# Another order for the second batch's loads, and the last batch's tokens in their own order

## The chip, the cores and the metric

The kernel runs on one core of a Trainium2 chip. A core has a matrix engine (TensorE, PE in the profile), a vector engine (VectorE, DVE), a scalar engine (ScalarE, ACT), a general engine (GpSimd, POOL) and a queue engine (SyncE, SP). Each engine works through a list of instructions of its own, in order, and waits on semaphores for the others. Transfers run on sixteen DMA engines; here POOL, SP and ACT issue them. Matrix results land in PSUM, all else lives in SBUF. The metric is the device time of one execution in microseconds (us); lower is better.

## The reference

Eight batches of eight heads, 576 tokens and a head size of 64. Thirty-two packing queries `p` per head first attend to the tokens, then the tokens attend to the 32 packed rows, and the result goes through a two-layer network with a smoothed ReLU.

```python
p_packed = sm_attn(p, k, v)              # softmax(p k^T / 8) v: 32 rows per head
out = sm_attn(q, p_packed, p_packed)     # softmax(q p_packed^T / 8) p_packed
x = out.transpose(0, 2, 1, 3).reshape(B * S, H * D)      # 4608 tokens x 512
h = x @ w_in                                              # 2048 wide
g = where(h >= 1, h, where(h <= -1, 0, (h + 1)**2 / 4))
return g @ w_out                                          # 4608 x 512, f32
```

All inputs and the output are f32; the kernel computes in bf16 with f32 sums.

## The kernel before, in words

The attention's last product and the first layer are joined. For each batch the packed rows (`ppT`) are multiplied with `w_in` (the tile `M`, made in four quarters `M0` to `M3` from the PSUM tile `mp`, L493), and the normalised second softmax (`A`) is multiplied with `M`, which gives a hidden tile `h` of 128 features by 576 tokens directly (L548). There are sixteen hidden tiles per batch. ACT and DVE turn each into `hT` in three passes (L553, L558 or L560, L563). The second layer runs for pairs of batches: 1152 tokens are nine output tiles `o` of 128 tokens, each a sum of sixteen output steps (L598), copied to `ob` and written by SP (L604). The last output tile is copied and written in two halves of its columns, one by ACT and one by DVE and SP (L612).

The attention of one batch runs like this. `k` and `q` are turned so that the head size lies on the partitions: in batches 0 to 2 by matrix transposes into PSUM (`tp`, L376) and copies to `kT` and `qT`, from batch 3 on by transposing DMAs that SP issues (L512). `scores` (L397) multiplies `kT` with `pT`, ACT takes the exp (L400), and `packed` (L417, L423) multiplies with `v` and sums. DVE and ACT then make `ppT` (copy, add, copy) and `rs` (reciprocals). In batch 0 `packed` runs once for each half of the heads, in all other batches once for both. `weights` multiplies `ppT` with `qT` (L451), takes the second exp into `eT` (L456), sums over the rows (`sm`, L461), takes the logarithm and its exp (L465, L469) and multiplies to `A` (L472). Heads 0 to 3 and 4 to 7 are the two groups of all this.

Loads are issued by POOL (L259 for k, q and v, which are converted to bf16 on the way; L285 and L287 for quarters of `w_in` and `w_out`). A load puts six neighbouring tokens on one partition, that is, partition p holds the tokens 6p to 6p + 5. So a batch's columns stand by token mod 6 first, and then by token div 6, and the rows of an output tile are written to `out` with a step of six rows, in pieces of up to 96 (`out_rows`).

The order of all instructions is written by a planner in the kernel (`Plan`) when the program is built. Each piece of work is a task with engines, a cost (the table `C`), a key and what it depends on; the planner keeps a clock for each engine, and gives each engine in turn the task that it can start first, or one with a smaller key if it can start nearly as soon. A task with two engines goes to the one that it thinks will end it first. Loads go out in the order in which they were added. PSUM has three wide buffers (`W`, used by `tp`, `sp`, `pk`, `s`, `sm`, `mp` and `h`) and two for output tiles (`O`), given out in rotation; a task that writes one waits for the readers of the old content. While fewer than three `O` buffers have been taken and PE has nothing to do, the planner lets it multiply zeros (L661). The costs only decide the order; at run time the engines wait on semaphores for what really happens.

```python
add_weights("in", 0); add_weights("in", 1); add_weights("out", 0); add_weights("in", 2)
add_weights("out", 1); add_weights("in", 3); add_weights("out", 2)
add_load("k", 1, 2); add_load("v", 1, 1); add_load("q", 1, 2)
add_weights("out", 3)
```

This is the order of the loads after those of batch 0 (here with several calls on a line): `add_load(name, batch, parts)`.

Of the kernel before, what the change touches and what calls it, by code (L numbers as in the profile page):

```python
# [8 lines left out]

C = dict(load=2.95, half=1.46, w_in=2.57, w_out=2.57, rest=1.25, out=9.0, p=4.05, land=1.75, xt=5.0, xland=11.0,
         tpp=0.06, tp=0.042, sc=0.034, pk=1.05, s2=0.25, sm=0.245, M=0.345, h=0.49, o=0.217, switch=0.05, join=0.15,
         pTc=0.1, Tca=1.12, Tcd=0.76, ex=0.82, ppT=0.42, ppo=0.41, ppa=0.4, ppd=0.2, rs=0.18, eT=0.74, ln=0.65, rc=0.68, A=0.82,
         Mca=1.0, Mcd=1.22, x=0.65, ta=0.683, td=0.457, hT=0.758, oba=0.585, obd=0.69,
# [17 lines left out]
class Plan:  # L33
# [15 lines left out]
    def add(self, engines, cost, key, deps, fn, takes=None, readers=0, frees=None, mode=None, slack=None, after=0.0,  # L49
            holds=0.0):  # L50
        engines = (engines,) if isinstance(engines, str) else engines
        t = Task(engines, cost if isinstance(cost, dict) else {e: cost for e in engines}, key, deps, fn, takes, readers,
                 frees, mode, slack, after, holds)
        t.seq = len(self.tasks)
        self.tasks.append(t)
        return t
# [124 lines left out]
def kernel(  # L181
# [10 lines left out]
    nc = tc.nc  # L192
    f32 = mybir.dt.float32
    bf16 = mybir.dt.bfloat16
    AF = mybir.ActivationFunctionType
    ALU = mybir.AluOpType

    B, H, S, D = q.shape
# [3 lines left out]
    P = 128  # L202
    assert d_model == H * D and n_tokens == B * S
    assert S == 576 and D == 64 and NP == 32 and H == 8 and d_ff == 2048 and B % 2 == 0
    scale = 1.0 / math.sqrt(D)
# [3 lines left out]
    G = 2  # L209
    Q = 4  # L210
    TP = 96
    NC = S // TP
    X = 2
    E = NC // X
    HALF = S // X
    KF = d_ff // P
    FW = 512
    NF = d_ff // FW
# [15 lines left out]
    PE, ACT, DVE, DMA, SP = "PE", "ACT", "DVE", "DMA", "SP"  # L234
# [42 lines left out]
    def add_load(nm, b, parts=1, deps=(), cost="load"):  # L277
        for i, hs in enumerate([ALL] if parts == 1 else HS):
            L[nm, b, i] = add(DMA, C[cost] / parts, -1, deps, lambda nm=nm, b=b, hs=hs: load(nm, b, hs))
        if parts == 1:  # L280
            L[nm, b, 1] = L[nm, b, 0]

    def add_weights(which, f):
        if which == "in":
            fn = lambda: nc.gpsimd.dma_start(w_in_sb[:, :, f * FW:(f + 1) * FW], w_in_v[:, :, f * FW:(f + 1) * FW])  # L285
        else:
            fn = lambda: nc.gpsimd.dma_start(w_out_sb[:, 4 * f:4 * f + 4], w_out_v[:, 4 * f:4 * f + 4])  # L287
        L[which, f] = add(DMA, C["w_" + which], -1, (), fn)
# [8 lines left out]
            load(nm, 0, HS[i])  # L297
    for nm, i in FIRST:
        L[nm, 0, i] = add(DMA, C["half"], -1, (), (lambda: None) if L else first_loads)
    add_weights("in", 0)  # L300
    add_weights("in", 1)
    add_weights("out", 0)
    add_weights("in", 2)
    add_weights("out", 1)
    add_weights("in", 3)
    add_weights("out", 2)
    add_load("k", 1, 2)
    add_load("v", 1, 1)
    add_load("q", 1, 2)
    add_weights("out", 3)  # L310
    L["p"] = add(DMA, C["rest"], -1, (), lambda: nc.gpsimd.dma_start(p_nat[:, PB * 2:], p_v[:, PB * 2:]))


# [43 lines left out]
    def attention(b, key):  # L357
# [46 lines left out]
        def packed(gs, deps):  # L404
            box, ky = {}, key["pk" + str(gs[0])]
            hs, n = slice(Q * gs[0], Q * gs[-1] + Q), Q * len(gs)
            part = 0.55 if len(gs) < G else 1.0

            def mm():
                pk = wide([P, 1024], f32, "pk")  # L410
                vt, ex_ = tok["v", b], ex()
                v_ = box["v"] = pk[:, :n * X * NP].rearrange("p (h y) -> p h y", h=n)
                for g in gs:
                    for a in range(Q):
                        h = head(g, a)
                        for e in range(E):
                            nc.tensor.matmul(v_[:, h - hs.start].rearrange("p (x n) -> p x n", x=X),  # L417
                                             vt[:, h, X * e:X * (e + 1)].rearrange("p c d -> p (c d)"), ex_[:, e, g, :, a],
                                             start=(e == 0), stop=(e == E - 1))
                s_ = box["s"] = pk[:, 512:512 + 2 * len(gs)].rearrange("p (g y) -> p g y", y=2)  # L420
                for i, g in enumerate(gs):
                    for c in range(NC):
                        nc.tensor.matmul(s_[:, i], ex_[:, c // X, g, c % X].rearrange("p a n -> p (a n)"), ones2[:TP],  # L423
                                         start=(c == 0), stop=(c == NC - 1))
            t = add(PE, C["pk"] * len(gs) / G, ky, [L["v", b, g] for g in gs] + deps + old("s2", "M", "A"), mm, takes="W",
                    readers=3, mode=0)
            war = old("s2", "M")

            def odd(eng):
                box["p1"] = att.tile([D, n, NP], f32, tag="p1", name="p1")  # L430
                copy(box["p1"], box["v"][D:, :, NP:])(eng)
            c1 = both(odd, C["ppo"] * part, C["ppo"] * part, ky, [t] + war, frees=t)
            c2 = add(DVE, C["ppT"] * part, ky, [c1] + war, lambda eng: nc.vector.tensor_tensor(
                ppT()[:D, hs], box["v"][:D, :, :NP], box["p1"], ALU.add), frees=t)
            res = [c2, both(lambda eng: copy(ppT()[D:, hs], ppT()[:D, hs])(eng), C["ppa"] * part, C["ppd"] * part, ky, [c2] + war)]
            r = add(DVE, C["rs"], ky, [t] + old("eT", "A"), lambda eng: nc.vector.reciprocal(
                rs()[:, gs[0]:gs[-1] + 1], box["s"]), frees=t)
            return t, res, r
# [4 lines left out]
        def weights(g, deps, r):  # L443
            box, ky, km = {}, key["s2" + str(g)], key["sm" + str(g)]

            def mm():
                s2 = box["s2"] = wide([P, X, FW], f32, "s2")
                for a in range(Q):
                    h = head(g, a)
                    for x in range(X):  # L450
                        nc.tensor.matmul(s2[a * NP:(a + 1) * NP, x, :HALF], pp_of(x, h),  # L451
                                         qT()[x * D:(x + 1) * D, g, h % 4 * E * TP:][:, :E * TP], start=True, stop=True)

            def exp2(eng):
                box["eT"] = att.tile([P, X, HALF], bf16, tag="eT", name="eT")
                nc.scalar.activation(box["eT"], box["s2"][:, :, :HALF], AF.Exp, scale=rs()[:, g, 1:])  # L456

            def mm2():
                sm = box["sm"] = wide([P, X, FW], f32, "sm")
                for x in range(X):  # L460
                    nc.tensor.matmul(sm[:, x, :HALF], onesblk, box["eT"][:, x], start=True, stop=True)  # L461

            def ln(eng):
                box["ln"] = att.tile([P, X, HALF], f32, tag="ln", name="ln", bufs=1)
                nc.scalar.activation(box["ln"], box["sm"][:, :, :HALF], AF.Ln)  # L465

            def inv(eng):
                box["rc"] = att.tile([P, X, HALF], f32, tag="rc", name="rc")
                nc.scalar.activation(box["rc"], box["ln"], AF.Exp, scale=-1.0)  # L469

            def norm(eng):
                nc.vector.scalar_tensor_tensor(A()[:, g], box["eT"], rs()[:, g, :1], box["rc"], ALU.mult, ALU.mult)  # L472
            p_ = K.get((b - 1, "A" + str(g)), [])
            t, j = yield ky, C["s2"], deps + p_, mm
            e_ = add(ACT, C["eT"], ky, [t, r] + p_, exp2, frees=(t, j))
            t2 = add(PE, C["sm"], km, [e_], mm2, takes="W", readers=1, mode=0)
            l_ = add(ACT, C["ln"], km, [t2] + last.get("ln", []), ln, frees=t2)
            i_ = add(ACT, C["rc"], km, [l_] + p_, inv)
            a_ = add(DVE, C["A"], km, [i_] + K.get((b - 2, "h"), []), norm)
            last["ln"] = [i_]  # L480
            K[b, "A" + str(g)] = [a_]
            yield t, e_, a_
# [39 lines left out]
        s1, e1 = scores(1, kc1 + pT_of[b])  # L522
        q0, qc0 = trans("q", 0, qT, old("s2"))
        q1, qc1 = trans("q", 1, qT, old("s2"))
        pk, pc, r = zip(*([packed((0,), [e0]), packed((1,), [e1])] if b == 0 else [packed((0, 1), [e0, e1])] * G))
        K[b, "sc"], K[b, "pk"] = [s0, s1], list(pk)
        K[b, "kt"], K[b, "qt"] = [k0, k1], [q0, q1]
        ws, ms = [weights(g, pc[g] + (qc0, qc1)[g], r[g]) for g in range(G)], [mk(f, pc[0] + pc[1]) for f in range(NF)]
# [44 lines left out]
    def out_rows(pr, i):  # L573
        res, t = [], i * P
        while t < (i + 1) * P:
            b, x, e, r = 2 * pr + t // S, t % S // HALF, t % HALF // TP, t % TP
            n = min(TP - r, (i + 1) * P - t)
            res.append((t - i * P, n, out[b * S:(b + 1) * S].rearrange("(p c) d -> c p d", c=NC)[X * e + x, r:r + n]))
            t += n
        return res  # L580

# [54 lines left out]
    keys = {0: {nm: -1 + 0.01 * i for i, nm in enumerate(names)}}  # L636
    for f in range(1, NF):
        keys[0]["M" + str(f)] = 0.25 * f - 0.12
    order = "kT0 kT1 sc0 qT0 sc1 qT1 pk0 s20 M0 s21 sm0 M1 sm1 M2 M3".split()
    for b in range(1, B):  # L640
        lo, hi = (b - 1 + 0.05, b - 0.05)
        keys[b] = {nm: lo + (hi - lo) * i / len(order) for i, nm in enumerate(order)}
# [49 lines left out]
```

## Time and profile before

| what | value |
|---|---|
| median of three runs | 251.23 us (250.75 to 251.34) |
| the profiled execution | 250.97 us, its span 249.2 us |
| PE busy | 234.8 us, 94% of the span |
| DVE and ACT busy | 181.7 and 182.5 us, 73% each |
| POOL busy | 29.7 us |
| read from HBM, written to it | 37.22 MB, 9.44 MB |
| granted TensorE clock | 1.00 |

The profile is one execution; the times of its lines count from the start of the span. An instruction's line names its source line, its engine, its operation and the tiles it writes and reads (out<-in), then how many of them follow each other. "Idle before" is the time in which its engine had nothing to do, with what ended it. Matmuls are pipelined and their ends are modelled, so that starts say more than lengths. A few matmul records are missing from the trace, which shows as a short hole in a row of equal matmuls.

### The profile page before, as it was taken

Reading aid. Unit: us, or ns where it says so; the run is one execution under the profiler, and the core shown is the slowest. Engines: PE = TensorE matmul, PEld = TensorE weight load, DVE = VectorE, ACT = ScalarE, POOL = GpSimd, SP = SyncE. Lnnn points to the kernel's source line nnn. Section 1 sums busy time; section 2 is a strip of 40 time slices with the busy share of each in tenths; the row PEclk is TensorE's granted clock in tenths of the full one; section 3 lists DMA queues with packets and bytes.
Section 4 is the critical chain, followed back from the end, with each engine's and each line's share of the span. In section 5 each row is a group of like instructions: output and inputs, shape, how many; then the busy total and the mean of one; then the engine's idle time right before and its main releaser. Section 6 shows DMA issues by size and latency. Waiting matters only on the chain.

```text
span 249.2 us, 5464 instructions
## 1 busy us (share of the span) xinstructions
PE 234.8 (94%) x2187; PEld 140.9 (57%) x2220; DVE 181.7 (73%) x308; ACT 182.5 (73%) x294; POOL 29.7 (12%) x44
## 2 busy tenths in 40 slices
PE   7887887999999999999999999999999999999993
PEld 5655465467546666556565656656556465544452
DVE  5456979788999899698979985998569878930000
ACT  3368888899888899798798984997859796841110
POOL 8632433012001301111101000000000000000000
PEclk9999999999999999999999999999999999999999
DMA  6999999999999999999999932312112112133223
GB/s 99 196 207 207 206 203 195 204 240 204 193 182 217 165 190 193 208 183 188 223 191 223 218 76 53 79 42 49 42 42 45 43 42 45 42 84 86 54 74 84
DMA packets 54825, 34.37 MB, mean 138 GB/s; under 512 B 27536, under 2 KB 50320, under 8 KB 54800
## 3 DMA queue, kind: packets, MB, share of 16 engines
q0 software_dynamic: 24672, 18.55, 49.9%
q1 hardware_dynamic: 29968, 15.34, 31.7%
q8 instruction: 17, 0.28, 0.4%
q10 hardware_dynamic: 160, 0.13, 0.2%
q14 instruction: 8, 0.07, 0.1%
HBM read 37.22 MB, written 9.44 MB: 187 GB/s over the span
## 4 chain that ended last, share of the span: by engine, by line
PE 76%; DMA 13%; ACT 3%; POOL 3%; issue 2%; DVE 2%; DVEq 0%; ACTq 0%; POOLq 0%
PE o L598 44%; PE h L548 22%; DMA w_in_sb<-in_moe_w_in_dram 7%; DMA q<-in_q_dram 6%; PE mp L493 3%; PE sp L397 2%; PE pk L417 1%; PE sm L461 1%; PE s L451 1%; PE tp L376 1%; DVE pT L319 1%; POOL w_in_sb L285 1%; ACT eT L456 1%; POOL k L259 1%; PE pk L423 1%
## 5 line engine op out<-in xcount | busy, mean ns | idle before, releaser
L598 PE MATMUL o<-w_out_sb,hT 128*128 128x512 bf16 (+1 forms) x559 | 135.6, 373 | 2.1 <-issue 1.1
L563 DVE SCALAR_TENSOR_TENSOR hT<-x 128x576 bf16<-128x576 f32 x128 | 93.2, 754 | 8.3 <-PE o L598 3.5
L598 PEld LDWEIGHTS <-hT 128*128 128x128 bf16 x592 | 56.1, 98 | 53.7 <-issue 4.8
L553 ACT ACTIVATE x<-h 128x576 f32<-128x576 f32 x128 | 77.2, 653 | 12.1 <-PE h L548 8.3
L548 PE MATMUL h<-A,M 128*128 128x288 bf16 x512 | 76.0, 286 | 1.4 <-ACT M L319 0.5
L548 PEld LDWEIGHTS <-M 128*128 128x128 bf16 x512 | 49.3, 98 | 24.1 <-ACT M L319 1.0
L558 DVE TENSOR_SCALAR x<-x 128x576 f32<-128x576 f32 x84 | 38.5, 459 | 11.8 <-ACT x L553 10.9
L319 ACT COPY ob<-o 128x512 f32<-128x512 f32 (+1 forms) x23 | 13.2, 576 | 32.1 <-PE o L598 32.1
L560 ACT ACTIVATE x<-x 128x576 f32<-128x576 f32 x44 | 29.4, 683 | 0.5
L319 DVE COPY ob<-o 128x512 f32<-128x512 f32 (+1 forms) x14 | 9.4, 669 | 25.8 <-PE o L598 25.7
L319 DVE CAST M<-mp 128x1024 bf16<-128x1024 f32 x16 | 19.4, 1218 | 2.8 <-PE mp L493 2.8
L319 ACT CAST M<-mp 128x1024 bf16<-128x1024 f32 x16 | 15.8, 1012 | 1.2 <-PE mp L493 1.2
L400 ACT ACTIVATE ex<-sp 96x768 bf16<-96x768 f32 x16 | 12.9, 806 | 3.2 <-PE sp L397 3.1
L472 DVE SCALAR_TENSOR_TENSOR A<-eT,rs,rc 128x576 bf16<-128x576 bf16 x16 | 13.0, 812 | 2.1 <-ACT rc L469 2.1
L259 POOL DMA_DIRECT2D k<-in_k_dram x10 | 7.5, 746 | 56.5 <-DMA kT<-k 40.0
L456 ACT ACTIVATE eT<-s,rs 128x576 bf16<-128x576 f32 x16 | 11.2, 736 | 2.8 <-PE s L451 2.6
L493 PE MATMUL mp<-w_in_sb,ppT 64*32 64x512 bf16 x256 | 10.7, 381 | 2.6 <-DMA w_in_sb<-in_moe_w_in_dram 2.2
L465 ACT ACTIVATE ln<-sm 128x576 f32<-128x576 f32 x16 | 10.4, 648 | 2.2 <-PE sm L461 2.1
L661 PE MATMUL o<-zeros 128*128 128x256 bf16 x68 | 10.6, 301 | 1.2 <-DVE zeros L247 1.2
L469 ACT ACTIVATE rc<-ln 128x576 f32<-128x576 f32 x16 | 10.9, 683 | 0.5
L259 POOL DMA_DIRECT2D q<-in_q_dram x10 | 7.6, 759 | 26.2 <-DMA qT<-q 12.7
L397 PEld LDWEIGHTS <-kT 128*128 128x128 bf16 x192 | 7.4, 98 | 2.6 <-DVE kT L319 0.6
(47 smaller groups left out, 114.4 us busy)
## 6 DMA issues: line engine op xcount, KB each, us to landing
out_dram<-ob SPq DMA_DIRECT2D x23, 192.0 KB, 2.5
v<-in_v_dram POOLq DMA_DIRECT2D x7, 576.0 KB, 18.4
k<-in_k_dram POOLq DMA_DIRECT2D x6, 576.0 KB, 12.4
q<-in_q_dram POOLq DMA_DIRECT2D x6, 576.0 KB, 14.0
out_dram<-ob SPq DMA_DIRECT2D x24, 128.0 KB, 2.8
w_in_sb<-in_moe_w_in_dram POOLq DMA_DIRECT2D x4, 512.0 KB, 14.7
w_out_sb<-in_moe_w_out_dram POOLq DMA_DIRECT2D x4, 512.0 KB, 16.8
out_dram<-ob SPq DMA_DIRECT2D x23, 64.0 KB, 2.0
```

The source lines that it names most:

```text
L259: nc.gpsimd.dma_start(tok[nm, b][:, hs].rearrange("p h c d -> p h (c d)"), SRC[nm][b, hs].rearrange("h (p c) d -> p h (c d)", c=NC))
L319: return lambda eng: nc.vector.tensor_copy(out_, in_) if eng == DVE else nc.scalar.copy(out_, in_)
L400: nc.scalar.activation(ex()[:, :, i].rearrange("p e x a n -> p e (x a n)"), box["sp"], AF.Exp, scale=scale)
L456: nc.scalar.activation(box["eT"], box["s2"][:, :, :HALF], AF.Exp, scale=rs()[:, g, 1:])
L472: nc.vector.scalar_tensor_tensor(A()[:, g], box["eT"], rs()[:, g, :1], box["rc"], ALU.mult, ALU.mult)
L493: nc.tensor.matmul(mp[a * NP:(a + 1) * NP, g], pp_of(y, h), w_in_sb[y * D:(y + 1) * D, h // 2, f * FW:(f + 1) * FW], start=True, stop=True)
L548: nc.tensor.matmul(h[:, hf, :HALF], T[b, "M"][:, g, fi * P:(fi + 1) * P], T[b, "A"][:, g, hf], start=(g == 0), stop=(g == G - 1))
L553: nc.scalar.activation(box["x"], box["h"][:, :, :HALF], AF.Prelu, bias=-1.0, alpha=0.5)
L558: nc.vector.tensor_scalar(x, x, 1.0, 0.0, ALU.add, ALU.max)
L560: nc.scalar.activation(x, x, AF.Relu, bias=1.0)
L563: nc.vector.scalar_tensor_tensor(hT[:, fi, col:col + S].rearrange("p (a t) -> p a t", a=2), box["x"], 1.0, box["x"], ALU.min, ALU.mult)
L598: nc.tensor.matmul(o, hT[:, fi, i * P:(i + 1) * P], w_out_sb[:, fi, cs], start=(fi == 0), stop=(fi == KF - 1))
```

## The change

Four things change.

- After batch 0's loads, the order is w_in quarters 0, 1, 2, w_out quarters 0, 1, then batch 1's first halves of k and v, its second half of k, w_in quarter 3, the second half of v, w_out quarter 2, both halves of q, and w_out quarter 3. Batch 1's v, so far one load, becomes two.
- `packed` runs in two halves for batch 1 too (`b < 2`), and the list of keys has a place for `pk1`. That list gives the keys of batches 1 to 7, so all its later places shift a little.
- The planner's cost of a full load falls from 2.95 to 2.7, and its time for a transposing DMA's landing rises from 11 to 18.
- In the last batch (`ORDERED`) the second exp reads its columns in the old order and writes them in the tokens' own order: value t of the part (x, e) goes to column 6t + 2e + x. All later tiles of that batch then have tokens in order, and `out_rows` writes up to 128 neighbouring rows in one piece.

```diff
-C = dict(load=2.95, half=1.46, w_in=2.57, w_out=2.57, rest=1.25, out=9.0, p=4.05, land=1.75, xt=5.0, xland=11.0,
+C = dict(load=2.7, half=1.46, w_in=2.57, w_out=2.57, rest=1.25, out=9.0, p=4.05, land=1.75, xt=5.0, xland=18.0,
...
+    ORDERED = (B - 1,)
...
-    add_weights("in", 0)
...
-    add_load("k", 1, 2)
-    add_load("v", 1, 1)
-    add_load("q", 1, 2)
-    add_weights("out", 3)
+    for nm in "i0 i1 i2 o0 o1 k0 v0 k1 i3 v1 o2 q0 q1 o3".split():
+        if nm[0] in "io":
+            add_weights({"i": "in", "o": "out"}[nm[0]], int(nm[1]))
+        else:
+            i = int(nm[1])
+            L[nm[0], 1, i] = add(DMA, C["half"], -1, (), lambda nm=nm, i=i: load(nm[0], 1, HS[i]))
...
-                nc.scalar.activation(box["eT"], box["s2"][:, :, :HALF], AF.Exp, scale=rs()[:, g, 1:])
+                eT, s2 = box["eT"], box["s2"][:, :, :HALF]
+                if b in ORDERED:
+
+                    eT = eT.rearrange("p y t -> p (y t)").rearrange("p (t e x) -> p x e t", x=X, e=E)
+                    s2 = s2.rearrange("p x (e t) -> p x e t", e=E)
+                nc.scalar.activation(eT, s2, AF.Exp, scale=rs()[:, g, 1:])
...
-        pk, pc, r = zip(*([packed((0,), [e0]), packed((1,), [e1])] if b == 0 else [packed((0, 1), [e0, e1])] * G))
+        pk, pc, r = zip(*([packed((0,), [e0]), packed((1,), [e1])] if b < 2 else [packed((0, 1), [e0, e1])] * G))
...
-            n = min(TP - r, (i + 1) * P - t)
-            res.append((t - i * P, n, out[b * S:(b + 1) * S].rearrange("(p c) d -> c p d", c=NC)[X * e + x, r:r + n]))
+            if b in ORDERED:
+                n = min(S - t % S, (i + 1) * P - t)
+                res.append((t - i * P, n, out[b * S + t % S:][:n]))
+            else:
+                n = min(TP - r, (i + 1) * P - t)
+                res.append((t - i * P, n, out[b * S:(b + 1) * S].rearrange("(p c) d -> c p d", c=NC)[X * e + x, r:r + n]))
...
-    order = "kT0 kT1 sc0 qT0 sc1 qT1 pk0 s20 M0 s21 sm0 M1 sm1 M2 M3".split()
+    order = "kT0 kT1 sc0 qT0 sc1 qT1 pk0 pk1 s20 M0 s21 sm0 M1 sm1 M2 M3".split()
```

More of the change, by code (lines that the diff above doesn't have):

```diff
@@ L299 @@
         L[nm, 0, i] = add(DMA, C["half"], -1, (), (lambda: None) if L else first_loads)
-    add_weights("in", 0)
[L301 to L306, printed above, removed]
-    add_load("k", 1, 2)
-    add_load("v", 1, 1)
-    add_load("q", 1, 2)
-    add_weights("out", 3)
+    for nm in "i0 i1 i2 o0 o1 k0 v0 k1 i3 v1 o2 q0 q1 o3".split():
[4 more added lines that the diff above has]
+            L[nm[0], 1, i] = add(DMA, C["half"], -1, (), lambda nm=nm, i=i: load(nm[0], 1, HS[i]))
     L["p"] = add(DMA, C["rest"], -1, (), lambda: nc.gpsimd.dma_start(p_nat[:, PB * 2:], p_v[:, PB * 2:]))
```

## The prediction

> **What bounds the kernel now.** I read the page first: busy shares and the forty slices.
>
> ```profile
> span 249.2 us, 5464 instructions
> PE 234.8 (94%) x2187; PEld 140.9 (57%) x2220; DVE 181.7 (73%) x308; ACT 182.5 (73%) x294; POOL 29.7 (12%) x44
> PE   7887887999999999999999999999999999999993
> ```
>
> TensorE (PE) is busy 94% of the span, and from the eighth slice (about 44 us) to the last every slice is a 9. So a change can save time in three ways only: less PE work, fewer holes in the first fifty microseconds, or a shorter tail after the last matmul. Next I read the busy time in stretches of 5 us (columns: stretch, its length, then busy us and instructions of PE, weight load, DVE, ACT, POOL, then clock and DMA).
>
> ```profile
> 20.00:25.00 5.00, 4.09 (x33) 2.91 (x30) 3.41 (x7) 4.80 (x9) 0.90 (x2) 1.00 1.24 207
> 25.00:30.00 5.00, 4.28 (x32) 2.39 (x33) 4.62 (x9) 3.86 (x7) 1.66 (x3) 1.00 1.24 206
> 30.00:35.00 5.00, 4.38 (x42) 2.41 (x40) 3.59 (x7) 3.95 (x7) 2.53 (x3) 1.00 1.30 202
> 35.00:40.00 5.00, 4.95 (x98) 4.02 (x97) 4.80 (x9) 4.48 (x8) 1.54 (x2) 1.00 1.32 206
> 40.00:45.00 5.00, 3.47 (x64) 1.84 (x63) 4.40 (x8) 4.13 (x7) 1.53 (x2) 1.00 1.56 191
> 45.00:50.00 5.00, 4.83 (x43) 2.67 (x43) 3.96 (x6) 3.99 (x6) 0.00 (x0) 1.00 1.32 204
> ```
>
> PE adds up to 26.0 of 30 us: 4.0 us idle, and that is all there is to win here. Before 20 us the order of instructions is the same in both programs, and so are the loads ahead of the first w_in quarter. The granted clock is 1.00 throughout. What PE waits for there stands in its order of time (start, length, work; in brackets the idle time and what ended it):
>
> ```profile
> 20.21 3.67 PE L548 MATMUL h<-A,M 128*128 128x288 bf16 x28
> 25.07 0.41 PE L493 MATMUL mp<-w_in_sb,ppT 64*32 64x512 bf16 x8 [0.98 <-DMA w_in_sb<-in_moe_w_in_dram]
> 28.51 1.64 PE L548 MATMUL h<-A,M 128*128 128x288 bf16 x12 [0.49 <-ACT M L319]
> 33.59 0.68 PE L376 MATMUL tp<-ident,k 96*128 96x96 bf16 x12 [0.51 <-DMA k<-in_k_dram]
> 40.86 0.68 PE L376 MATMUL tp<-ident,q 96*128 96x96 bf16 x12 [0.58 <-DMA q<-in_q_dram]
> 42.44 0.32 PE L451 MATMUL s<-qT,ppT 64*32 64x288 bf16 x8 [0.43 <-DVE qT L319]
> 46.24 2.97 PE L598 MATMUL o<-w_out_sb,hT 128*128 128x512 bf16 x13
> 50.72 0.66 PE L548 MATMUL h<-A,M 128*128 128x288 bf16 x4 [0.29 <-DVE pT L319]
> 52.17 0.65 PE L548 MATMUL h<-A,M 128*128 128x288 bf16 x4
> ```
>
> Most of these waits are for a landing. The POOL queue shows the landings: each issue waits for the load issued eight before it, and starts some 0.28 us after that load has landed (first line, of the chain: the fourth weight's load lands at 8.14 + 16.89 = 25.03, and the issue that waited for it starts at 25.31).
>
> ```profile
> 8.14 16.89 DMA w_in_sb<-in_moe_w_in_dram
> ...
> 16.93 0.67 POOL L259 DMA_DIRECT2D k<-in_k_dram  x1 [2.35 <-DMA w_in_sb<-in_moe_w_in_dram]
> 19.44 0.78 POOL L259 DMA_DIRECT2D v<-in_v_dram  x1 [1.83 <-DMA w_in_sb<-in_moe_w_in_dram]
> 21.98 0.68 POOL L259 DMA_DIRECT2D q<-in_q_dram  x1 [1.76 <-DMA w_out_sb<-in_moe_w_out_dram]
> 25.31 0.67 POOL L259 DMA_DIRECT2D q<-in_q_dram  x1 [2.65 <-DMA w_in_sb<-in_moe_w_in_dram]
> 27.25 0.75 POOL L287 DMA_DIRECT2D w_out_sb<-in_moe_w_out_dram  x1 [1.28 <-DMA w_out_sb<-in_moe_w_out_dram]
> 32.59 0.78 POOL L259 DMA_DIRECT2D k<-in_k_dram  x1 [1.61 <-DMA w_out_sb<-in_moe_w_out_dram]
> DMA to landing us min/median/max: 16.1/16.1/16.1
> ```
>
> So the loads land one after the other: quarters of the weights at 16.65, 19.15, 21.7, 25.0, 27.0, later ones up to some 32; then batch 1's k from 33.5, and its last q half at 40.8. The last w_out quarter, issued at 27.25, lands 16.1 us later, at 43.35 (last line: issue to landing of that one).
>
> **The change, part by part.** *(1) The new order of loads.* Ahead of q the same bytes are fetched in another order, so q's two halves and the last w_out quarter keep their places: 40.8 and 43.35. What moves, by the landings above, one place for one place: the third w_in quarter goes from 25.0 to 21.7, the first w_out quarter from 21.7 to 25.0, batch 1's first k half from 33.5 to about 28.4 (fifth weight at 27.0, and half a quarter's time more), and v is cut in two, which adds one issue on POOL (0.67 twice for 0.78, beside its waits of 1.3 to 2.7 us).
>
> I follow PE's new list against these times. Seven hidden tiles run to 23.7 as before; M's third quarter then runs at once, and PE waits for w_out instead: 1.0 us, the old 0.98 under another name. One output step, a hidden tile and seven steps take it to 27.3. Next in its list stands the transpose of k, which lands at 28.4: 1.1 us of waiting with two ready hidden tiles behind it, in place of the old 0.49 (for M) and 0.51 (for k). Then come smaller waits: 0.5 for the last w_in quarter, 0.35 for the second half's exp, 0.4 for each half of q. Batch 1's packing by halves brings scores, packing and three of the M quarters forward, ahead of the last q. But at 43.35 PE has done all that can be done without the last w_out quarter in both programs, but for a matter of one M quarter. After that ACT has, in order, both exps, a logarithm, its exp, then two output copies that now stand ahead of the second logarithm; so the second A ends near 48.9 instead of 47.07 (its 46.25 plus 0.82), and ACT's three copies of pT after it hold a PSUM buffer until about 50.5. PE meanwhile has output steps, waits some 0.2 us for batch 2's k (issued at 32.59, about 47.5 on the chip by 14.9 us to landing) and 0.5 us for that buffer.
>
> ```profile
> L259 POOL DMA_DIRECT2D k<-in_k_dram x1: 778/778/778, 32.6 to 32.6; - x1
> DMA to landing us min/median/max: 14.9/14.9/14.9
> 160.27 1.96 PE h L548 x16
> 192.00 3.45 PE o L598 x16
> ```
>
> At 52.2 us I find the changed list 1 hidden tile ahead (three of batch 1 done, before: two) and 1 output step behind (42, before 43): 4 x 1.96/16 = 0.49, less 3.45/16 = 0.22, is a gain of 0.27 us. The bounds: at best the waits between 27 and 43 us shrink to what the late q and w_out force and those after 43 us go, 1.5 us; at worst my 1.1, 0.5, 0.35, 0.4, 0.4 and 0.5 run a third longer and no hidden tile is gained: 0.8 us lost. I take -0.27, the walk's own value.
>
> *(2) Split packing.* Each of the copies, adds and reciprocals of batch 1 becomes two of half the width:
>
> ```profile
> L319 ACT COPY p<-pk 64x256 f32<-64x256 f32 x6 | 2.2, 368 | 2.0 <-PE pk L423 1.9
> L319 ACT COPY p<-pk 64x128 f32<-64x128 f32 x2 | 0.5, 262 | 2.0 <-PE pk L423 2.0
> ```
>
> Twice 262 for 368 ns is 0.16 us more, and as much again for the add and the second copy: about 0.5 us on ACT and DVE together, which are idle for 0.2 to 1.6 us in each 5 us above. It is in the walk.
>
> *(3) Planner costs and keys.* The new landing cost of a transposed load only moves work within batches 3 to 7. After 50 us PE's slices are full, and at the end of batch 2's hidden tiles the new list has done 117 output steps (131 before) of the 208 that are open by then, so PE has a stock to draw on: nothing gained, nothing lost. SP's transposes stand between the same output writes but for a place or two.
>
> *(4) The tail.* The last tile's rows lie together, so each of its two queues issues one write instead of two:
>
> ```profile
> 245.25 0.37 ACT L319 COPY ob<-o 128x256 f32<-128x256 f32 x1 [2.75 <-PE o L598]
> 245.81 0.79 SPq L612 DMA_DIRECT2D out_dram<-ob  x2
> DMA to landing us min/median/max: 1.9/2.0/2.1
> ```
>
> The second write on SP starts some 0.37 us after the first and lands last. One write from 245.8 lands at 247.9 instead of 248.2. It is a third larger than the larger of the old two, so I take 0.3 of the 0.37; the bounds are 0.1 and 0.4. The other writes saved on SP (four tiles at one instead of two) lie beside PE, and no transpose is queued behind them.
>
> *(5) The permuted exp.* Batch 7's two exps write each value 12 bytes from the last one. The work around them, unchanged in its order:
>
> ```profile
> L456 ACT ACTIVATE eT<-s,rs x2: 732/736/740, 195.8 to 196.4; 128x576 bf16<-128x576 f32 x2
> 195.78 1.37 ACT L456 ACTIVATE eT<-s,rs 128x576 bf16<-128x576 f32 x2
> 197.06 0.41 PE L461 MATMUL sm<-eT,onesblk 128*128 128x288 bf16 x2
> 197.74 0.41 PE L461 MATMUL sm<-eT,onesblk 128*128 128x288 bf16 x2
> ```
>
> No row shows a write in such steps. The nearest is the exp itself, 736 ns, which I take as unchanged; the upper bound is a doubling. The exps end at 196.5 and 197.15, the sums that read them start at 197.06 and 197.74, so each pair has 0.4 us to spare. If one exp grows by d, PE, which keeps its order, stands for 2d - 0.4: 1.1 us for a doubling. The Trainium skill speaks against this part: SBUF — State Buffer, under "Door 1: The DMA port swizzle", says that each access that goes on to another 16-byte line pays a penalty, and that two hits a line are needed for full rate. By that rule nearly every write here would pay; a doubling would make my total 1.1 us worse. No trace here shows it.
>
> **The sum.** Against the profiled execution's 250.97 us (span 249.2): -0.27 - 0.3 + 0 = 250.4. The runs' median of 251.23 stands 0.26 above that execution, so 250.7 for the changed kernel. What this kernel's measurement can tell from no change is about 0.3%, 0.75 us: the forecast is a small gain inside that.
>
> **The rivals.** *Faster.* The waits shrink to what the last q and w_out force: speaks for it that k, v and the M quarters are all early, against it that those two keep their times. 1.5 and 0.3 from 251.23 is 249.4. Chance 0.40.
> *Slower, by the late start of batch 1.* Place: ACT between 44 and 51 us. If the second logarithm behind two output copies delays the first hidden tile by more than the open output steps cover, PE stands. It starts at 50.6 by my walk, at 49.05 before; should that difference of 1.5 us stay uncovered on top of the 0.5 that I counted, the time is 250.7 + 1.5 = 252.2. It decides from 1.3 us of uncovered delay. Against it: 13 output steps ran in one stretch at 46.24, and as many are open. Chance 0.11.
> *Slower, by the exp.* A tripling (d = 1.47) gives 2.5 us: 253.2; from d = 0.85 on it decides. Chance 0.07.
> *The forecast*, within 0.3%: chance 0.42, with a range of its own of 250.5 to 251.9.
>
> The range of 249.3 to 252.2 takes in the first rival and the late start, and leaves the exp's tripling out. Faster 0.40, same 0.42, slower 0.18.
>
> **What would show it.** Right: the PE list of the changed profile has a wait for k near 27.3 to 28.4, M quarters of batch 1 before 41 us, a first hidden tile of batch 1 near 50, eT near 0.74 us in the last batch, and one write on each queue at the end. Wrong: 20 to 50 us with under 2.8 us of PE idle time (the faster rival) or over 5.3; or eT over 1.5 us near 196.

## The result, and the profile after

The changed kernel is slower: 254.53 us in the median (253.57 to 255.41), against 251.26 for the kernel before; the ratio is 1.0134, with a 95% interval of 1.0092 to 1.0175. The forecast of 250.7, and its range up to 252.2, were wrong. The profiled execution of the changed kernel took 255.41 us with a span of 253.6.

```profile
span 253.6 us, 5478 instructions
PE 240.6 (95%) x2220; PEld 141.9 (56%) x2220; DVE 180.1 (71%) x309; ACT 188.3 (74%) x297; POOL 30.1 (12%) x45
PE   7978799999999999999999999999999799999993
PEclk9999999999999999999999999999999899999998
```

The page of the changed kernel has two marks that were not there before: a 7 in PE's row of slices at about 200 us, and an 8 in the granted clock beside it. (The 8 in the last slice lies behind PE's last matmul.) PE's order of time at that place, first of the changed kernel and then of the kernel before (start, length, work, and idle time with its cause; one M quarter behind the scores is left out of both):

```profile
196.05 0.44 PE L447 MATMUL s<-qT,ppT 64*32 64x288 bf16 x16
196.64 1.25 PE L603 MATMUL o<-w_out_sb,hT 128*128 128x512 bf16 x5
198.68 0.41 PE L462 MATMUL sm<-eT,onesblk 128*128 128x288 bf16 x2 [0.78 <-ACT eT L457]
198.92 0.59 PE L603 MATMUL o<-w_out_sb,hT 128*128 128x512 bf16 x2
200.60 0.53 PE L462 MATMUL sm<-eT,onesblk 128*128 128x288 bf16 x2 [1.08 <-ACT eT L457]
200.92 3.19 PE L603 MATMUL o<-w_out_sb,hT 128*128 128x512 bf16 x7
204.04 0.86 PE L494 MATMUL mp<-w_in_sb,ppT 64*32 64x512 bf16 x24
```

```profile
195.39 0.44 PE L451 MATMUL s<-qT,ppT 64*32 64x288 bf16 x16
196.20 1.03 PE L598 MATMUL o<-w_out_sb,hT 128*128 128x512 bf16 x4 [0.16 <-issue]
197.06 0.41 PE L461 MATMUL sm<-eT,onesblk 128*128 128x288 bf16 x2
197.31 0.59 PE L598 MATMUL o<-w_out_sb,hT 128*128 128x512 bf16 x2
197.74 0.41 PE L461 MATMUL sm<-eT,onesblk 128*128 128x288 bf16 x2
197.99 1.67 PE L598 MATMUL o<-w_out_sb,hT 128*128 128x512 bf16 x7
199.59 0.84 PE L493 MATMUL mp<-w_in_sb,ppT 64*32 64x512 bf16 x24
```

The work is the same, in the same order; of the five output steps ahead of the first sum, the trace of the kernel before has four, and a hole where the fifth is missing. From the last batch's scores to the second sum PE took 4.55 us (196.05 to 200.60), before 2.35 (195.39 to 197.74): 2.20 us more, all of it waiting for ACT's two exps. From there to the M matmuls it took 3.44 us, before 1.85, without any wait: seven output steps took 3.19 us instead of 1.67, each 0.43 instead of 0.22. The exps of the last batch, and the granted clock in stretches of the changed kernel (the clock stands two columns before the last):

```profile
L457 ACT ACTIVATE eT<-s,rs x2: 2183/2239/2295, 196.4 to 198.2; 128x576 bf16<-128x576 f32 x2
196.44 4.10 ACT L457 ACTIVATE eT<-s,rs 128x576 bf16<-128x576 f32 x2
...
195.00:197.50 2.50, 2.50 (x34) 0.95 (x32) 1.76 (x3) 2.42 (x4) 0.00 (x0) 1.00 0.38 105
197.50:200.70 3.20, 1.33 (x7) 0.58 (x6) 2.30 (x4) 3.20 (x3) 0.00 (x0) 1.00 0.00 0
200.70:203.90 3.20, 3.20 (x9) 0.99 (x7) 2.13 (x3) 2.34 (x4) 0.00 (x0) 0.51 0.01 3
```

The permuted exp takes 2239 ns instead of 736, three times as long; the two together, which overlap a little, take 4.10 us instead of 1.37. Behind PE's two waits the clock was halved for some 3.4 us: 1.6 us more. Of the 4.4 us by which the span grew, 2.2 + 1.6 = 3.8 lie here; 0.66 us of lateness was there already at the scores (0.21 of it before the first hidden tile, at 20.42 instead of 20.21).

In the early part the waits that the walk named are there, in their order; whether its gain came is told further down:

```profile
25.22 0.38 PE L603 MATMUL o<-w_out_sb,hT 128*128 128x512 bf16 x1 [0.79 <-DMA w_out_sb<-in_moe_w_out_dram]
29.11 0.68 PE L372 MATMUL tp<-ident,k 96*128 96x96 bf16 x12 [1.51 <-DMA k<-in_k_dram]
34.58 0.41 PE L494 MATMUL mp<-w_in_sb,ppT 64*32 64x512 bf16 x8 [0.31 <-DMA w_in_sb<-in_moe_w_in_dram]
48.24 1.19 PE L372 MATMUL tp<-ident,k 96*128 96x96 bf16 x24 [0.16 <-DMA k<-in_k_dram]
51.48 1.83 PE L549 MATMUL h<-A,M 128*128 128x288 bf16 x12 [0.54 <-DVE kT L315]
```

### The profile page after: what moved, and what is told of

The parts are those of the page before. It is cut to its first block, busy times and chain, and to the rows that moved or that the text cites. A ratio compares the mean times of both kernels' runs of the same rounds, so it can differ in the third digit from the quotient of the medians.

```text
span 253.6 us, 5478 instructions
## 1 busy us (share of the span) xinstructions
PE 240.6 (95%) x2220; PEld 141.9 (56%) x2220; DVE 180.1 (71%) x309; ACT 188.3 (74%) x297; POOL 30.1 (12%) x45
## 4 chain that ended last, share of the span: by engine, by line
PE 77%; DMA 15%; ACT 4%; DVE 1%; issue 1%; POOL 0%; POOLq 0%
PE o L603 46%; PE h L549 22%; DMA q<-in_q_dram 8%; DMA w_out_sb<-in_moe_w_out_dram 7%; PE mp L494 2%; PE pk L413 2%; PE sp L393 2%; ACT eT L457 2%; PE sm L462 1%; PE s L447 1%; ACT rc L470 1%; ACT ln L466 1%; PE tp L372 1%; PE pk L419 1%; ACT pT L315 1%
## 5 line engine op out<-in xcount | busy, mean ns | idle before, releaser
L603 PE MATMUL o<-w_out_sb,hT 128*128 128x512 bf16 (+1 forms) x592 | 144.5, 377 | 0.8 <-DMA w_out_sb<-in_moe_w_out_dram 0.8
L549 PE MATMUL h<-A,M 128*128 128x288 bf16 x512 | 75.0, 286 | 0.8 <-DVE kT L315 0.5
L559 DVE TENSOR_SCALAR x<-x 128x576 f32<-128x576 f32 x89 | 41.4, 466 | 15.7 <-ACT x L554 15.1
L315 ACT COPY ob<-o 128x512 f32<-128x512 f32 (+1 forms) x25 | 14.3, 576 | 30.3 <-PE o L603 30.2
L561 ACT ACTIVATE x<-x 128x576 f32<-128x576 f32 x39 | 26.3, 684 | 0.3
L315 DVE COPY ob<-o 128x512 f32<-128x512 f32 (+1 forms) x12 | 8.0, 666 | 25.9 <-PE o L603 25.8
L315 DVE CAST M<-mp 128x1024 bf16<-128x1024 f32 x14 | 17.1, 1221 | 5.4 <-PE mp L494 5.3
L315 ACT CAST M<-mp 128x1024 bf16<-128x1024 f32 x18 | 17.6, 1013 | 2.6 <-PE mp L494 2.3
L457 ACT ACTIVATE eT<-s,rs 128x576 bf16<-128x576 f32 x16 | 14.0, 928 | 2.9 <-PE s L447 2.8
L260 POOL DMA_DIRECT2D v<-in_v_dram x10 | 7.3, 730 | 16.2 <-PE pk L419 13.0
```

The source lines that it names most:

```text
L260: nc.gpsimd.dma_start(tok[nm, b][:, hs].rearrange("p h c d -> p h (c d)"), SRC[nm][b, hs].rearrange("h (p c) d -> p h (c d)", c=NC))
L315: return lambda eng: nc.vector.tensor_copy(out_, in_) if eng == DVE else nc.scalar.copy(out_, in_)
L457: nc.scalar.activation(eT, s2, AF.Exp, scale=rs()[:, g, 1:])
L549: nc.tensor.matmul(h[:, hf, :HALF], T[b, "M"][:, g, fi * P:(fi + 1) * P], T[b, "A"][:, g, hf], start=(g == 0), stop=(g == G - 1))
L559: nc.vector.tensor_scalar(x, x, 1.0, 0.0, ALU.add, ALU.max)
L561: nc.scalar.activation(x, x, AF.Relu, bias=1.0)
```

## The experiments

The theory from the two profiles: the exp's writes in steps of 12 bytes make all of the loss, by PE's wait and by the half clock behind it. The rival: the new loads and planner costs lose it, by the order that they leave behind. All ratios are to the kernel before, run beside each kernel on the same chip.

**The change without its permuted exp.**

```diff
-    ORDERED = (B - 1,)
+    ORDERED = ()
```

> The changed kernel without the permuted exp: the last batch keeps the old token order and the old output writes; new loads, split packing, keys and costs stay. Theory 1 (the permuted exp costs all of the loss, through PE's wait and a half-speed clock behind it): eT of the last batch back at 0.74 us, no wait before its sums, no stretch of half clock; 251.3 to 252.0 us (before 251.26, and 0.5 us for the early part, by which the last batch's scores start later: 196.05 against 195.39). Theory 2 (the early part and the order it leaves behind cost it): 253 us or more.

Measured: 251.39 us, ratio 0.9989 (0.9966 to 1.0011). No loss is left; the rival, as a cause of the loss, falls.

**The permuted exp alone**, in the kernel before: `ORDERED`, the exp and `out_rows` of the change, nothing else.

> The kernel before, with nothing of the change but the permuted exp and the output rows that go with it. Theory 1: eT of the last batch 2.2 us, PE idle 0.8 and 1.1 us before the two sums, then some 3.4 us at half clock; 251.26 + 2.2 + 1.7 - 0.3 = 254.9, and 253.2 where the clock does not drop. Theory 2: 251.0 to 251.3 us, the tail's gain alone.

Measured: 254.52 us (253.13 to 255.11), ratio 1.0103 (1.0056 to 1.0151). It makes a loss of nearly the same size by itself. But in this profile (254.16 us) the half clock does not stand where the theory has it:

```profile
43.60:47.00 3.40, 3.40 (x29) 0.73 (x28) 2.67 (x3) 2.51 (x4) 0.00 (x0) 0.50 1.36 203
201.20:204.60 3.40, 3.40 (x38) 1.35 (x36) 2.45 (x4) 3.31 (x6) 0.00 (x0) 1.00 0.05 15
```

From the scores to the second sum PE took 4.55 us again (196.43 to 200.98), with the same two waits (0.79 and 1.08). Behind them the clock stayed at 1.00; it was halved at 44 us, long before the last batch. So in this profile the exp cost the 2.20 us of waiting, and the rest of the loss lay elsewhere.

**Work in the wait.** Zeros multiplied into the sum's PSUM tile, ahead of the sum:

```diff
                 sm = box["sm"] = wide([P, X, FW], f32, "sm")
+                for _ in range((9, 11)[g] if b in ORDERED else 0):
+                    nc.tensor.matmul(sm[:, 0, :DW], zeros[:, :P], zeros[:, :DW], start=True, stop=True)
```

> The changed kernel, with 9 and 11 multiplications of zeros (0.11 us each) on PE ahead of the last batch's two sums, where it waited. The wait for the exps stays, PE is busy in it. Theory A (PE's idle time brings the half clock): granted clock 1.00 right after the sums, output steps 0.216 us each, 254.53 less the 1.7 us of half clock: 252.8 us. Theory B (the clock drops for a reason of its own): the stretch of 0.5 is there as before, 254.5 us.

Measured: 254.88 us, ratio 1.0124 (1.0084 to 1.0164).

```profile
198.19 1.14 PE L462 MATMUL sm<-zeros 128*128 128x256 bf16 x9 [0.78 <-ACT eT L457]
199.16 0.41 PE L464 MATMUL sm<-eT,onesblk 128*128 128x288 bf16 x2
200.12 1.36 PE L462 MATMUL sm<-zeros 128*128 128x256 bf16 x11
201.32 0.41 PE L464 MATMUL sm<-eT,onesblk 128*128 128x288 bf16 x2
```

The edit misses its aim: the zeros themselves wait for the exp, because the sum's PSUM buffer is the one that held the scores, which the exp has to read first. The nine fill what was PE's second wait, and the eleven come on top: from the scores to the second sum it takes 5.76 us (195.56 to 201.32), 1.21 more than in the changed kernel. With one wait of 0.78 us left, the clock stayed at 1.00 in this profile. Both times that were expected are missed, and the run alone does not tell theories A and B apart.

**The exp priced.**

```diff
-            e_ = add(ACT, C["eT"], ky, [t, r] + p_, exp2, frees=(t, j))
+            e_ = add(ACT, 2.25 if b in ORDERED else C["eT"], ky, [t, r] + p_, exp2, frees=(t, j))
```

> The changed kernel, with the planner told what the permuted exp takes (2.25 us instead of 0.74), so that it puts 12 and 9 output steps ahead of the two sums instead of 5 and 2. Theory 1: 1.5 us more of work ahead of each sum covers the waits of 0.8 and 1.1 us, the clock stays at 1.00; 254.53 - 2.0 - 1.7 = 250.8 us, with eT still 2.2 us. Rival: the later A holds up the hidden tiles, the stall only moves to the first hidden tile: 252.5 us or more.

Measured: 251.39 us, ratio 0.9987 (0.9962 to 1.0011), with the slow exp still in it:

```profile
L457 ACT ACTIVATE eT<-s,rs x2: 2193/2253/2313, 196.0 to 197.8; 128x576 bf16<-128x576 f32 x2
196.22 2.76 PE L603 MATMUL o<-w_out_sb,hT 128*128 128x512 bf16 x12
198.82 0.41 PE L462 MATMUL sm<-eT,onesblk 128*128 128x288 bf16 x2
199.07 2.11 PE L603 MATMUL o<-w_out_sb,hT 128*128 128x512 bf16 x9
201.01 0.41 PE L462 MATMUL sm<-eT,onesblk 128*128 128x288 bf16 x2
```

With 12 and 9 output steps ahead of the sums PE has no wait. So the 2.7 us more on ACT cost nothing that can be measured; what cost was that the written order did not know of them.

**Reading in the new order, writing without gaps**, in the kernel before with `ORDERED` and `out_rows`:

```diff
+                if b in ORDERED:
+                    eT = eT.rearrange("p y t -> p (y t)").rearrange("p (t e x) -> p t e x", x=X, e=E)
+                    s2 = s2.rearrange("p x (e t) -> p t e x", e=E)
```

> The kernel before, with the last batch's tokens put in their own order by the second exp in the other way: it reads its PSUM tile in the new order (neighbouring values a bank or 96 values apart) and writes eT without gaps. The output is the same as in the changed kernel. Theory W (the 12-byte steps of the write cost the time): eT at 0.74 us, no wait before the sums; 251.0 us, before's 251.37 less up to 0.3 for the tail. Theory P (a pattern with three inner dimensions, or a jumping read, costs it): eT at 2.2 us or more, 253 to 255 us.

Measured: ratio 0.9982 (0.9958 to 1.0005), median 251.31, beside 252.00 for the kernel before; the exps took 732 and 740 ns. The same values in the same places, and only the side of the jumps is another: jumps in the PSUM read are free here, jumps in the SBUF write are not.

**The order made one step later, by DVE.** Each A of the last batch is written in 12-byte steps, in two instructions:

```diff
+                    a = a.rearrange("p y t -> p (y t)").rearrange("p (t e x) -> p x e t", x=X, e=E)
...
+                for x in range(X) if b in ORDERED else [slice(None)]:
+                    nc.vector.scalar_tensor_tensor(a[:, x], eT[:, x], rs()[:, g, :1], rc[:, x], ALU.mult, ALU.mult)
```

> The kernel before, with the last batch's tokens put in order one step later, by DVE: the two A of the last batch are written in 12-byte steps, each by two instructions of 288 values. Theory W for any engine (SBUF takes 12-byte steps slowly): A goes from 0.82 us to some 2.3 us per group, the hidden tiles of the last batch start 1.5 to 3 us later, PE waits for them: 252.5 us or more. Theory W for ACT alone: two pieces of 0.4 to 0.6 us per group, 251.0 to 251.4 us.

Measured: 253.66 us, ratio 1.0064 (1.0039 to 1.0090).

```profile
L478 DVE SCALAR_TENSOR_TENSOR A<-eT,rs,rc x4: 1156/1226/1274, 199.9 to 203.3; 128x288 bf16<-128x288 bf16 x4
204.66 0.40 PE L554 MATMUL h<-A,M 128*128 128x288 bf16 x2 [1.77 <-DVE A L478]
```

Two halves at 1226 ns make 2.45 us per group instead of 0.81: DVE pays for the steps as ACT does, and PE waits for A.

**What a step costs.** A probe; its kernel is not whole, as the expectation says.

```diff
+                eT, s2, k = box["eT"], box["s2"][:, :, :HALF], (1, 2, 4, 6, 8, 12, 16, 32)[b]
+                if k > 1:
+                    eT = eT.rearrange("p y t -> p (y t)").rearrange("p (t e x) -> p x e t", x=X, e=k // X)
+                    s2 = s2.rearrange("p x (e t) -> p x e t", e=k // X)
```

> A probe on the kernel before: the second exp of batches 1 to 7 writes eT in steps of 4, 8, 12, 16, 24, 32 and 64 bytes (batch 0 without gaps), reading in the old order; so the output rows of these batches come out in another order, and its time is not that of a whole kernel. Per exp, theory L (what counts is how many values of two bytes fall in a line of 16 bytes; two or more are free): 0.74 us at steps of 4 and 8 bytes, about 2.2 us at 12, the same or a little more from 16 on. Theory G (any gap costs): 2.2 us at 4 bytes already. Theory R (short inner runs cost; they are 288, 144, 96, 72, 48, 36 and 18 values long): a steady growth to the last, under 2.2 us at 8 bytes and far over it at 64.

The two exps of each batch, from batch 0 on (shortest, median and longest in ns, and when):

```profile
L460 ACT ACTIVATE eT<-s,rs x2: 740/740/741, 12.0 to 16.3; 128x576 bf16<-128x576 f32 x2
L460 ACT ACTIVATE eT<-s,rs x2: 892/900/907, 42.3 to 43.1; 128x576 bf16<-128x576 f32 x2
L460 ACT ACTIVATE eT<-s,rs x2: 1547/1550/1553, 68.6 to 69.9; 128x576 bf16<-128x576 f32 x2
L460 ACT ACTIVATE eT<-s,rs x2: 2168/2228/2288, 88.6 to 90.4; 128x576 bf16<-128x576 f32 x2
L460 ACT ACTIVATE eT<-s,rs x2: 2818/2934/3049, 113.7 to 116.0; 128x576 bf16<-128x576 f32 x2
L460 ACT ACTIVATE eT<-s,rs x2: 2827/2944/3062, 142.1 to 144.4; 128x576 bf16<-128x576 f32 x2
L460 ACT ACTIVATE eT<-s,rs x2: 2692/2793/2894, 180.0 to 182.2; 128x576 bf16<-128x576 f32 x2
L460 ACT ACTIVATE eT<-s,rs x2: 2791/2894/2996, 212.4 to 214.7; 128x576 bf16<-128x576 f32 x2
```

In steps of 2, 4, 8, 12 and 16 bytes: 0.74, 0.90, 1.55, 2.23 and 2.93 us; beyond 16 bytes it grows no more (2.94, 2.79, 2.89). None of the three theories has it right. It grows steadily with the number of pieces of 16 bytes that the 576 values are spread over as they are written: 144, 288, 432 and 576 at 4, 8, 12 and 16 bytes, and 576 from there on. From 288 to 576 pieces it grows by 1.38 us, 4.8 ns a piece. The gapless write touches 72 pieces and takes 0.74 us, so there another limit holds. Theory R falls by the last rows (the inner runs go from 72 to 18 values, the time does not grow), theory G by the small cost at 4 bytes, theory L because two values a piece are not free.

**Longer exps without gaps.** The last batch takes each second exp twice or three times, in the kernel before:

```diff
-                nc.scalar.activation(box["eT"], box["s2"][:, :, :HALF], AF.Exp, scale=rs()[:, g, 1:])
+                for _ in range(2 if b == B - 1 else 1):
+                    nc.scalar.activation(box["eT"], box["s2"][:, :, :HALF], AF.Exp, scale=rs()[:, g, 1:])
```

> The kernel before, whose last batch takes each second exp twice (the same values again, written without gaps), so d = 0.74 us per exp. By the prediction's working PE stands 2d - 0.4 = 1.1 us. Theory A (the clock halves where PE idles long enough; 1.1 us in two pieces is too short): clock 1.00, 251.37 + 1.1 = 252.4 us, runs close together. Theory B (any such wait brings the half clock): 252.4 + 1.7 = 254 us in most runs.

> The kernel before, whose last batch takes each second exp three times, all without gaps: 2.2 us per group as in the changed kernel. If the length of the exps alone made the loss, by PE's wait and the half clock behind it: PE idle some 0.8 and 1.1 us before the sums, 253.3 us in runs at full clock and up to 255 where it drops, as with the 12-byte writes (254.5). If the gaps in eT slow its readers too (the sums on PE, A on DVE): about 1 us less than that.

Measured: twice 252.64 us, ratio 1.0041 (1.0014 to 1.0068); three times 254.14 us (253.63 to 254.76), ratio 1.0100 (1.0067 to 1.0133). With three exps:

```profile
199.37 0.41 PE L462 MATMUL sm<-eT,onesblk 128*128 128x288 bf16 x2 [0.89 <-ACT eT L457]
201.55 0.40 PE L462 MATMUL sm<-eT,onesblk 128*128 128x288 bf16 x2 [1.34 <-ACT eT L457]
201.50:204.90 3.40, 3.35 (x37) 1.41 (x37) 2.11 (x3) 3.31 (x5) 0.00 (x0) 1.00 0.00 0
44.00:47.40 3.40, 3.07 (x29) 0.70 (x23) 2.77 (x3) 2.38 (x4) 0.00 (x0) 0.50 1.35 204
```

With two exps PE took 1.01 us more than before from the scores to the second sum (195.83 to 199.19), close to the 1.1 us of the prediction's working (2d - 0.4), and the clock stayed at 1.00 there. With three it took 2.56 us more, and the time is nearly that of the 12-byte writes. So the length of the exps is what counts; that the readers of eT are slowed does not show. The lines above, of the kernel with three exps, show that waits longer than the changed kernel's (0.89 and 1.34) need not bring the half clock: it stayed at 1.00 behind them, and was halved once elsewhere, at 44 us, behind the waits of the early part.

**The whole change, with the reading exp.** The two `rearrange` lines of the reading exp in the changed kernel.

> The whole changed kernel, with the second exp of the last batch reading in the new order and writing without gaps. If the 12-byte writes were all of the loss: eT 0.74 us, clock 1.00, and the time of the changed kernel without its permuted exp (251.39 beside 251.37), less up to 0.3 for the tail: 251.0 us. If more was lost elsewhere: 252 us or more.

Measured: 251.20 us, ratio 0.9984 (0.9961 to 1.0008). All of the loss is gone. It beats the changed kernel; against the kernel before the interval holds 1.

**All batches ordered by reading**, in the kernel before.

```diff
+    ORDERED = tuple(range(B))
```

> The kernel before, with all eight batches put in their own order by the reading exp, so that every output tile is written in pieces of up to 128 neighbouring rows. If the writes in pieces hold nothing up but the last: 251.0 us, as with the last batch alone. If the 35 or so issues saved on SP bring the transposing loads forward where PE waits for them: 250 us; there was no such wait in before's profile, so I expect the first.

Measured: 251.43 us, ratio 0.9997 (0.9971 to 1.0022). In the medians fewer output writes gain nothing. But 7 of the 12 executions have a mean granted clock below 0.995; the other five took 250.75 us in the median, against 251.19 for the kernel before in its 18 executions of that kind. What the tail has to do with these 0.4 us is told below.

**The new loads and packing with the old planner costs.**

```diff
-    ORDERED = (B - 1,)
+    ORDERED = ()
...
-C = dict(load=2.7, ... xland=18.0,
+C = dict(load=2.95, ... xland=11.0,
```

> The kernel before with the new order of loads, the split packing of batch 1 and the new key, and with the old planner costs and the old last batch. By the prediction's walk through 20 to 52 us: 0.27 us less than before (251.1); its bounds 1.5 us less to 0.8 us more. Against the run without the permuted exp (0.9989 of before), which has the new costs too, it shows what these did: by the prediction nothing, 0.2 us or less.

Measured: 252.15 us, ratio 1.0030 (1.0008 to 1.0053): 0.75 us slower, outside what a gain of 0.27 allows and at the prediction's bound of 0.8 us. With the new costs (the first run) the ratio is 0.9989. The two intervals overlap by 0.0003, but of twelve executions each, the slowest with the new costs (251.78) is about as fast as the fastest with the old ones (251.70); the kernel before took 251.37 beside both. The profiles say where it is lost. From the first hidden tile of batch 1 to ACT's copy of the last output tile it took 194.44 us with the new costs (51.62 to 246.06), and 195.32 with the old ones (50.89 to 246.21): 0.88 us, all of it behind the early part. One place that shows is PE's weight loads (PEld), which stand three times between 126 and 160 us ahead of a hidden tile, and with the new costs nowhere there:

```profile
126.88 2.30 PEld L549 LDWEIGHTS <-M 128*128 128x128 bf16 x19 [0.28 <-issue]
132.28 0.34 PEld L549 LDWEIGHTS <-M 128*128 128x128 bf16 x3 [0.47 <-issue]
159.38 0.34 PEld L549 LDWEIGHTS <-M 128*128 128x128 bf16 x3 [0.39 <-issue]
```

## Why the prediction was wrong

**The permuted exp (part 5) is the step that failed.** Its working was right in kind: the place, and the formula 2d - 0.4 for PE's wait. The term that it mis-sized was d, the growth of one exp. I took d as 0 because the nearest row was the gapless exp, and bounded it by a doubling for no better reason than that it seemed large; d measured 1.50 us (2239 instead of 736 ns). The formula then gives 2.6 us, and PE's wait measured 2.20. The rows close that gap: the two exps overlap, so that together they grew by 2.73 us (4.10 less 1.37), not by 3.0; and the second sum, which used to start 0.59 us after the exps' end (197.74 less 197.15), now starts 0.06 after it (200.60 less 200.54), so that 0.53 us was to spare, not 0.4. 2.73 - 0.53 is 2.20. The prediction's own sign of being wrong, an eT of over 1.5 us near 196, came true. "A tripling", with 253.2 us, stood among the rivals at a chance of 0.07 and outside the range. The page of the Trainium skill that I cited (SBUF — State Buffer, "Door 1: The DMA port swizzle") spoke against the change, and the runs agree with its direction. Its line of 16 bytes is what the probe found; its word that two hits a line are enough for full rate does not hold here: at two values a line the exp took 1.55 us instead of 0.74.

**The half clock was in none of the rivals.** In the changed kernel's profile it explains what lies beyond the wait: 1.6 us. Of the four timed executions, the one whose mean granted clock was 1.00 took 253.57, and the three at 0.990 to 0.993 took 254.19 to 255.41. So 253.57 - 251.26 = 2.3 us is about the price of the wait, by one execution, and the rest up to the median goes with the clock.

Whether the waits bring it was not settled. In all the profiles together the clock is halved seven times while PE works, each time for some 3.4 us and each time behind a stretch in which PE stood for a good part: it was busy for 1.33 of 3.20 us in the changed kernel, for 2.04 of 3.40 in the run without the permuted exp (at 13 us), and for 1.98 of 3.40 with the permuted exp alone (at 44 us, where the order made by DVE and the three exps have it too). The other two stand in the probe of steps, behind two of the five pairs of waits that its long exps bring. But such stretches also pass at full clock: the other three pairs of the probe, the same waits as the changed kernel's in the permuted exp alone, and 1.98 of 3.40 us busy at 40.2 to 43.6 in the kernel before. So the waits seem to be needed, and are not enough.

The timed executions say how often. One stretch of 3.4 us at half clock takes the mean over 250 us to about 0.993 (an estimate), so executions below 0.995 can be counted. The kernel before has 34 of them in 81 beside the experiments: 252.18 us in the median, against 251.19 in the other 47. With the new loads and no wait at the exps (the run without the permuted exp, the priced one, the reading exp in the changed kernel, the old costs) it is 3 of 48; in the changed kernel it is 3 of 4, and with the zeros in the wait 1 of 6. That speaks for the waits as the cause in the changed kernel, but the clock was not forced on and off by an experiment.

**New order of loads (part 1).** Predicted 0.27 us gained, with bounds from -1.5 to +0.8. The waits came out near the walk's: 0.79 for w_out (1.0), 1.51 for k (1.1), 0.31 for w_in (0.5), 0.16 and 0.54 at the end (0.2 and 0.5). The first hidden tile of batch 1 started at 51.48, or 51.27 less the later start, by the walk 50.6. But the hidden tile by which the walk was ahead is missing. Its third tile of batch 1 was to be done at 52.2; in this profile the third starts at 52.66, before at 52.17. The output steps done by then are 42 and 43, as in the walk. So by its own count the changed kernel is 0.7 us late there (0.49 and one step of 0.22), 0.2 of it since the first hidden tile, where the walk has it 0.27 ahead; this is about the 0.66 us of lateness at the last scores. Four other profiles with the new loads, at full clock, have the third tile at 52.07 to 52.23: 0.1 to 0.3 us late by the same count. Of batch 1's M quarters two, not three, stand ahead of 41 us.

Loads, packing and costs together measured 0.9989 (0.9966 to 1.0011), that is 0.3 us gained, give or take 0.6: the forecast lies in it, and so does nothing at all, and by the lines above it would lie there by luck. At full clock there is no gain: 251.25 us in the median of eleven executions, 251.19 in the 47 of the kernel before. What these runs do show of the new loads is the count above: 3 of 48 executions with a lowered clock instead of 34 of 81. The prediction did not think of it, and the faster rival (chance 0.40) falls.

**Planner costs (part 3).** "Nothing gained, nothing lost" is in doubt: by the run with the old costs, the new loads with these are 0.3% slower than the kernel before. So the new costs, which I set at nothing, carry some 0.9 us, by the 0.88 us between the two profiles.

**Tail (part 4).** The writes did what was said, and the end of the program took most of it back. SP issues one, and it lands some 2.1 us later:

```profile
250.13 0.42 ACTq L617 DMA_DIRECT2D out_dram<-ob  x1
250.29 0.33 SPq L617 DMA_DIRECT2D out_dram<-ob  x1
DMA to landing us min/median/max: 1.9/2.0/2.1
```

The last write landed 2.55 us after the end of PE's last matmul, before 2.89: 0.34 us gained (predicted 0.3). But from there to the end of the span it took 1.28 us instead of 1.00. SP checks at the end, one after another, whether all its DMAs have landed, some 0.06 us each; before, the last landing was checked next to last, and now six checks follow it. What is left is 0.06 us. Where all batches are ordered the last landing falls late in the checks again (1.04 us to the end), so this is a matter of which semaphore the last write happens to have. There the tail, from the end of PE's last matmul to the end of the span, is 3.49 us, against 3.83 in the changed kernel and 3.88 before: 0.39 us gained, as predicted in kind and size, and most of what that run had at full clock.

**Split packing (part 2)** cannot be told apart from part 1 by these runs.

## What to carry to other kernels

Put a permutation on the side where the engine jumps for free: here the same exp took 0.74 us when it jumped in reading PSUM and 2.24 when it jumped in writing SBUF. When an operation's cost changes in a kernel with a written order, the order must be told: with the true price in the planner, the same slow exp cost nothing. And where no row bounds a cost, the range must hold what a documented penalty could do, not a round factor of two.

## What was not expected of the hardware

- In the probe a write of two-byte values in steps cost by the number of 16-byte pieces touched, about 4.8 ns each on ACT between 288 and 576 pieces; steps of 4 bytes already cost 0.16 us, and the cost grew no more once there was one value a piece. DVE's 288 values in 12-byte steps (216 pieces) took 1226 ns, 5.7 ns a piece if all of it is put down to them.
- The clock was halved for 3.4 us behind two waits of 0.78 and 1.08 us, with PE busy for 1.33 of 3.20 us between. The Trainium skill (TensorE: Matmul & The Clock Gate, "Why this matters for your kernels") warns of idle gaps over some 3 us; in these traces only shorter ones stood ahead of it, and in the profile of the permuted exp alone the same waits (0.79 and 1.08) passed at full clock. What decides it was not tried.
- The end of the program can hide a gain of 0.3 us in the order in which landings are checked.
